# Hash attention with a PReLU layer on one core: first three weights on SyncE behind pair 1's blocks, weight 0's passes later, sums of x behind the next divide

## Chip, core and metric

The kernel runs on one core of a Trainium2 chip. A core has five engines with instruction streams of their own: TensorE (PE, matmuls), VectorE (DVE), ScalarE (ACT), GpSimd (POOL) and SyncE (SP, which here only issues DMAs). They meet through semaphores. The metric is device time in microseconds. The kernel before has a median of 879.39 us over three runs (879.0 to 880.38).

## The reference, cut to what matters

```python
# q, k, v: (4, 8, 768, 64), proj: (64, 6)
q_bits = (q @ proj > 0); k_bits = (k @ proj > 0)      # a bucket of 6 bits per row
mask = q_bucket[:, :, :, None] == k_bucket[:, :, None, :]
scores = where(mask, q @ k.T / sqrt(64), -1e9)
attn = softmax(scores); x = (attn @ v)                 # heads side by side: x is (3072, 512)
h = x @ w_in                                           # w_in (512, 2048)
g = max(h, 0) + alpha * min(h, 0)
out = g @ w_out                                        # w_out (2048, 512)
```

The weights arrive as 64-bit floats and are used as 32-bit floats.

## The kernel before

**Pairs and cells.** The 32 (batch, head) problems are taken two heads at a time, in 16 pairs: pair `pi` is batch `pi // 4`, heads `2 * (pi % 4)` and the next. The loop over pairs fills the first 325 us or so; the two matrix products with the weights fill the rest. Within a pair, `scores` (L760 to L771) goes through 12 cells: six blocks of 128 keys (`kc`) by two halves of 384 queries (`g`). A cell is six matmuls into one two-bank PSUM tile `sc`, and one exponential on ScalarE into `pt`. The tag `sc` has three such tiles, and `totals` (the sums `sm` of the softmax, L815), the transposes of the first pair and the hash products take theirs from the same three, in turn. So a pair's third cell gets the tile that the preceding pair's `sm` held, once the two `st` transposes at the head of `divide` (L831) have read it.

**Order.** `do` keeps each engine's instructions in the order in which the program lists them. All engines run strictly in that order. The steps of one turn of the loop over pairs on VectorE are:

1. `divide(pi - 1, weight_begin)`: the `st` transposes, reciprocals, then, by `weight_begin`, `turn_blocks` of the next k, the clamp and parts of weight `2 pi`, `add_first` (L779, needs the first four exponentials of the pair in the order of the loop); then `dn` and `x` (L843, L849);
2. `weight_sum` of weight `2 pi` (two operations), the clamp of the next weight, `add_third`, the two of `add_last`, and `add_total`;
3. the parts and the sum of weight `2 pi + 1`, `turn_blocks` of the q two pairs on;
4. in pairs 11, 12, 13 and 15 one of the four sums of x (`sum_x`, L874, which subtracts two blocks of x of 128 x 768).

TensorE has, in a turn: 12 cells, the hash products of the next pair, `attend` (96 matmuls, 7.96 us) and `totals`, which needs `add_total`.

**Weights.** There are 32 weight pieces of 512 KB, two a pair. `load_weight(i)` (L578 to L582) issues the load, on the POOL queue if nothing else is said, into one of three `raw` buffers. `weight_abs(i)` (L591 to L600) takes the pieces apart: a pass on ScalarE (`wr`, L596), and another on ScalarE or, if so told, on VectorE (`wx`, L598). `weight_clamp` (L606) and `weight_parts` (L612) follow on VectorE, then `weight_sum` (L637, L640). POOL makes combinations of finished pieces (L659), one for each call of `weight_sums`.

**The start.** Pair 0's q and k are loaded in two halves each: q on SP's queue, k on ScalarE's. The first half is turned by TensorE (L695), copied and hashed; so is the second. From pair 1 on, q and k come by blocks of 32 columns (`load_blocks`, L512: four DMAs of 96 KB for each, in runs of 128 bytes) and are turned by VectorE (`turn_blocks`, L704). `ahead` names the three cells of pair 0 that need only the first half of q and k. The first of them lies between the second halves' transposes and their hash products.

The order of loads on SP after setup: second half of q0; weight 0; q1; k1; v0; v1; q2; k2. Weights 1 and 2 go out on POOL's queue, which reaches them as soon as its setup is done.

```python
    load_weight(0, nc.sync)
    load(1, "q")
    load(1, "k")
    load(0, "v")
    for i in range(1, 3):
        load_weight(i)
```

Of the kernel before, what the change touches and what calls it, by code (L numbers as in the profile page):

```python
# [407 lines left out]
def fast_path(  # L408
# [12 lines left out]
    nc = tc.nc  # L421
# [22 lines left out]
    PE, DVE, ACT, POOL = nc.tensor, nc.vector, nc.scalar, nc.gpsimd  # L444
# [38 lines left out]
    def load(pi, name):  # L483
        b, hp = pairs[pi]
        src = {"q": q, "k": k, "v": v}[name]
        if name == "v":
            t = pool.tile([P, 2, NC * D], F32, name=f"vn{pi}", tag="vn")
            nc.sync.dma_start(t, src[b, 2 * hp : 2 * hp + 2].rearrange("h (p c) d -> p h (c d)", c=NC))
            nat[name, pi] = t
        elif pi and name in BY_BLOCKS:  # L490
            load_blocks(pi, name)
        else:
            load_part(pi, name, slice(0, NC), nc.sync)
# [84 lines left out]
    def load_weight(i, queue=nc.gpsimd):  # L578
        if i < NW:
            i = order[i]  # L580
            raw[i] = pool.tile([P, 512], moe_w_in.dtype, name=f"raw{i}", tag="raw", bufs=3)
            queue.dma_start(raw[i], piece(i))  # L582
# [8 lines left out]
    def weight_abs(i, engine=None):  # L591
        i = order[i]
        lo, hi = halves(i)
        wx[i] = pool.tile([P, 512], F32, name=f"wx{i}", tag="wx")
        wr[i] = pool.tile([P, 512], I32, name=f"wr{i}", tag="wr")
        do(ACT.activation(wr[i], lo, AF.Copy, scale=2.0 ** -29))  # L596
        if engine is DVE:
            do(DVE.tensor_scalar(wx[i].bitcast(U32), hi, 0x7FFFFFFF, None, op0=ALU.bitwise_and))  # L598
            return
        do(ACT.activation(wx[i], hi.bitcast(F32), AF.Abs))  # L600

    def weight_clamp(i):
        if i < NW:
            i = order[i]
            x = wx[i]
            do(DVE.tensor_scalar(x, x, HI_MIN, None, op0=ALU.max, op1=ALU.max, accum_out=wmax[:, i : i + 1]))  # L606

    def weight_parts(i):
        i = order[i]
        x = wx[i].bitcast(U32)  # L610
        turned = i < HW and i % 4 == 3
        do(DVE.tensor_scalar(  # L612
            x, x, 3, 0x40000000 if turned else 0xC0000000, op0=ALU.logical_shift_left, op1=ALU.bitwise_xor,
        ))

    def weight_sum(i):


        i = order[i]
        lo, hi = halves(i)  # L620
        x = wx[i]
        if i < HW:
            n, m = divmod(i, 4)
            if m == 0:
                wst[n] = pool.tile([P, NM, 4, P], F32, name=f"wsi{n}", tag="wsi")
            slot = (0, 5, 1, 2)[m]
            dst = wst[n][:, slot].rearrange("p i f -> p (i f)")
        else:
            n, m = divmod(i - HW, 2)
            if m == 0:  # L630
                wst[HW + n] = pool.tile([P, 4, DM // 2], F32, name=f"wso{n}", tag="wso")
            w = wst[HW + n]
            dst = w[:, 0:4:3] if m == 0 else w[:, 1:3]
        x, r = x.bitcast(I32), wr[i]
        if i >= HW:
            hi, x, r = (t.rearrange("p (a f) -> p a f", a=2) for t in (hi, x, r))
        do(DVE.scalar_tensor_tensor(  # L637
            x.bitcast(U32), hi, 0x80000000, x.bitcast(U32), op0=ALU.bitwise_and, op1=ALU.bitwise_xor,
        ))
        do(DVE.tensor_tensor(dst.bitcast(I32), x, r, op=ALU.add))  # L640
        return (dst if i < HW else dst[:, 0])[:, :1]
# [118 lines left out]
    def scores(pi, cells):  # L760
        for kc, g in cells:
            sc = two_banks(f"sc{pi}_{kc}_{g}")
            ks = slice(kc * P, (kc + 1) * P)
            qs = slice(g * CW, (g + 1) * CW)
            for what, first in ((bits, True), (tr, False)):
                for s in range(2):
                    r = slice(D * s, D * s + D)
                    do(PE.matmul(  # L768
                        sc[:, s, :CW], what["k", pi][r, ks], what["q", pi][r, qs], start=first, stop=not first,
                    ))  # L770
            do(ACT.activation(pts[kc][:, g, :, :CW], sc[:, :, :CW], AF.Exp, scale=SCALE / DOWN))  # L771
# [5 lines left out]
    def add_first(pi):  # L777
        accp[pi] = pool.tile([P, 2 * NCH, CW], F32, name=f"accp{pi}", tag="accp", bufs=1)
        do(DVE.tensor_tensor(accp[pi], p(0), p(1), op=ALU.add))  # L779
# [40 lines left out]
    def divide(pi, between=lambda: None):  # L820

        b, hp = pairs[pi]
        n = HW2 // 32
        a = pool.tile([P, NCH, HW2], F32, name=f"st{pi}", tag="st", bufs=1)
        r = pool.tile([P, NCH, n], F32, name=f"rc{pi}", tag="rc")
        rr = pool.tile([P, NCH, 2, n], F32, name=f"rr{pi}", tag="rr")
        d = pool.tile([P, NCH, CW], F32, name=f"dn{pi}", tag="dn", bufs=1)
        for g in range(NCH):  # L830
            do(DVE.transpose(a[:, g], sums[pi][:, g, :HW2]))  # L831
        do(DVE.tensor_scalar(r, a.rearrange("p g (n w) -> p g n w", w=32)[:, :, :, 0], S * EPS, None, op0=ALU.add))
        for h in range(2):
            do(DVE.reciprocal(rr[:, :, h], r))
        vsum[pi] = pool.tile([P, 1], F32, name=f"vs{pi}", tag="vs")
        do(DVE.tensor_scalar(vsum[pi], av[pi][:, 0, CW : CW + 1], EPS, None, op0=ALU.mult))
        weight_sums(1, vsum[pi])
        for q0 in (0, D):
            q1 = q0 + 32
            do(POOL.tensor_copy(rr[q0 : q0 + 32, :, 1], rr[q1 : q1 + 32, :, 1]))  # L840
            do(POOL.tensor_copy(rr[q1 : q1 + 32, :, 0], rr[q0 : q0 + 32, :, 0]))
        between()
        do(DVE.transpose(  # L843
            d.rearrange("p g w -> p (g w)"),
            rr.rearrange("p g h n -> p (g h n)").unsqueeze(2).to_broadcast([P, 2 * NCH * n, 32]),
        ))

        x = mid.tile([P, NCH, CW], F32, name=f"x{pi}", tag="x", bufs=1)
        do(DVE.scalar_tensor_tensor(x, av[pi][:, :, :CW], vsum[pi], d, op0=ALU.add, op1=ALU.mult))  # L849
        nc.sync.dma_start(x_s[b, hp], x.rearrange("p g w -> p (g w)"))  # L850
# [291 lines left out]
    for half in (first, second):  # L1142
        turn(0, "q", half)
        turn(0, "k", half, DVE)
        if half is first:
            nil[0]()
            hash_bits(0, first, DVE)
    load_weight(0, nc.sync)
    load(1, "q")
    load(1, "k")  # L1150
    load(0, "v")
    for i in range(1, 3):
        load_weight(i)
    load(1, "v")
    load(2, "q")
    load(2, "k")
# [1 line left out]
    ahead = [(kc, 0) for kc in range(CH)]  # L1158
# [3 lines left out]
    turn_blocks(1, "q")  # L1162
    turn_blocks(1, "k")

    weight_abs(0, DVE)
    weight_clamp(0)
    weight_parts(0)
    for pi in range(NPAIR):
        i = 2 * pi

        def weight_begin():
            if pi + 1 < NPAIR:
                turn_blocks(pi + 1, "k")
            weight_clamp(i)
            weight_parts(i)
            add_first(pi)

        scores(pi, [c for c in CELLS if pi or c not in ahead])
        if pi:
            divide(pi - 1, weight_begin)  # L1180
        else:
            add_first(pi)
        weight_sum(i)
        weight_group(i)
        load_weight(i + 3)
        if pi == 0:
            weight_abs(1, DVE)
        weight_clamp(i + 1)
        add_third(pi)
        add_last(pi)  # L1190
        add_total(pi)
        weight_parts(i + 1)
        weight_sums(1, weight_sum(i + 1))
        weight_group(i + 1)
        load_weight(i + 4)
        if pi + 1 < NPAIR:
            hash_bits(pi + 1)
            do(ACT.activation(tr["q", pi + 1], tr["q", pi + 1], AF.Copy, scale=DOWN))
        if pi + 2 < NPAIR:
            turn_blocks(pi + 2, "q")  # L1200
        attend(pi)
        if pi + 1 == NPAIR:
            now = ff1(0, 0)
            now.step(1)
        totals(pi)
        if pi + 1 == NPAIR:
            now.step(5)
            divide(pi)
        else:
            weight_abs(i + 2)  # L1210
        if pi + 2 < NPAIR:
            load(pi + 2, "v")
        if pi in (9, 11, 15):
            load_w((9, 11, 15).index(pi))
        if pi in (9, 10, 12):
            load_x(0, *{9: (0,), 10: (2, 3), 12: (1,)}[pi])
        if 11 <= pi < 14 or pi == 15:
            sum_x(0, min(pi - 11, 3), DVE)
        if pi == 1:
            setup_alpha()  # L1220
        for name in "qk":
            magnitude(pi, name)
            if pi + 3 < NPAIR:
                load(pi + 3, name)
        if pi + 1 < NPAIR:
            weight_abs(i + 3)
# [97 lines left out]
```

## Time and profile before

| | |
|---|---|
| median of 3 runs | 879.39 us |
| the profiled execution | 879.32 us |
| its span, first to last instruction | 877.4 us |
| mean granted TensorE clock | 0.996 |
| DMA | 137.23 MB, mean 156 GB/s |

The durations below all come from the one profiled execution. Its span leaves out 1.9 us around the instructions. A row of the time line gives start, length, engine, line, what is written from what, how often, and in brackets how long the engine had been idle and what ended that. A row of the waits gives total, number of times and the longest. Times are microseconds from the start of the span.

The first pair on VectorE, in the order of time:

| start us | what | length us |
|---|---|---|
| 14.98 | second half's bits of k (L755) | 1.37 |
| 16.38, 17.28 | `turn_blocks` of q1 and k1 | 0.98, 0.94 |
| 18.14 | `weight_abs(0)` | 0.38 |
| 18.56 | clamp of weight 0 | 0.69 |
| 19.29 | parts of weight 0 | 0.43 |
| 19.76 | `add_first(0)` | 1.76 |
| 21.44 | `weight_sum(0)` | 0.68 + 0.69 |
| 29.15 | `add_total(0)` | 1.76 |
| 33.61 | `st` of pair 0 | 0.61 |

On ScalarE the pass of weight 0 (L596, 0.68 us) starts at 17.65, after the third exponential. On TensorE, `attend(0)` starts at 24.84, `totals(0)` at 32.61 and the third cell of pair 1 at 35.01.

### The profile page before, as it was taken

Reading aid. Unit: us, or ns where it says so; the run is one execution under the profiler, and the core shown is the slowest. Engines: PE = TensorE matmul, PEld = TensorE weight load, DVE = VectorE, ACT = ScalarE, POOL = GpSimd, SP = SyncE. Lnnn points to the kernel's source line nnn. Section 1 sums busy time; section 2 is a strip of 40 time slices with the busy share of each in tenths; the row PEclk is TensorE's granted clock in tenths of the full one; section 3 lists DMA queues with packets and bytes.
Section 4 is the critical chain, followed back from the end, with each engine's and each line's share of the span. In section 5 each row is a group of like instructions: output and inputs, shape, how many; then the busy total and the mean of one; then the engine's idle time right before and its main releaser. Section 6 shows DMA issues by size and latency. Waiting matters only on the chain.

```text
span 877.4 us, 15248 instructions
## 1 busy us (share of the span) xinstructions
PE 861.8 (98%) x5706; PEld 574.8 (66%) x5706; DVE 749.7 (85%) x1215; ACT 368.5 (42%) x654; POOL 117.6 (13%) x251
## 2 busy tenths in 40 slices
PE   7999999999999999999999999999999999999996
PEld 3444444444444445559996558996558997557996
DVE  4999999999999987999897769898668889668985
ACT  5888788888777752221112222112222112222111
POOL 1223343323424401120000000000000000000000
PEclk9999999999999999999999999999999999999999
DMA  9775797898799437686434435333434433420242
GB/s 198 149 177 139 168 225 170 167 235 226 187 229 200 138 126 264 225 282 224 162 111 106 151 104 184 115 137 101 151 111 155 148 112 103 173 84 1 96 160 61
DMA packets 170819, 137.23 MB, mean 156 GB/s; under 512 B 126016, under 2 KB 154384, under 8 KB 167152
## 3 DMA queue, kind: packets, MB, share of 16 engines
q1 hardware_dynamic: 158672, 107.39, 43.2%
q0 software_dynamic: 9648, 27.60, 10.7%
q10 hardware_dynamic: 2416, 1.18, 0.5%
q8 instruction: 47, 0.77, 0.4%
q14 instruction: 36, 0.29, 0.1%
HBM read 104.87 MB, written 28.31 MB: 152 GB/s over the span
## 4 chain that ended last, share of the span: by engine, by line
PE 63%; DVE 5%; issue 1%; POOL 0%; ACT 0%; DVEq 0%; ACTq 0%
PE f_0a L902 2%; PE z_4a L902 2%; PE z_7a L902 2%; PE z_3a L902 2%; PE z_6a L902 2%; PE z_5a L902 2%; PE f_4a L902 2%; PE f_3a L902 2%; PE f_2a L902 2%; PE f_1a L902 2%; PE z_2a L902 2%; PE f_5a L902 2%; PE sc L768 2%; PE av L801 2%; PE z_1a L902 2%; PE f_7a L902 2%
## 5 line engine op out<-in xcount | busy, mean ns | idle before, releaser
L771 ACT ACTIVATE pt<-sc 128x768 f32<-128x768 f32 x192 | 154.2, 812 | 6.8 <-PE sc L768 5.3
L768 PE MATMUL sc<-qT,kT 64*128 64x384 f32 x768 | 155.8, 484 | 0.0
L801 PE MATMUL av<-pt,vn 128*32 128x385 f32 (+1 forms) x1536 | 127.4, 486 | 0.0
L801 PEld LDWEIGHTS av<-pt,vn 128*32 128x32 f32 x1536 | 48.7, 109 | 77.5 <-issue 68.7
L768 PEld LDWEIGHTS sc<-qT,kT 64*128 64x128 f32 x768 | 68.3, 188 | 37.9 <-issue 37.7
L955 DVE TENSOR_TENSOR g<-g,g 128x384 f32<-128x384 f32 x128 | 68.3, 554 | 2.2
L768 PE MATMUL sc<-qb,kb 64*128 64x384 bf16 x384 | 63.1, 324 | 2.3 <-DVE st L831 2.3
L1019 DVE TENSOR_TENSOR gs<-g,gs 128x768 f32<-128x768 f32 x56 | 53.3, 951 | 1.0
L1011 DVE TENSOR_TENSOR ws<-wl 128x512 f32<-128x512 f32 x56 | 38.4, 686 | 17.9 <-DMA wl<-w_out_s 16.1
L1019 DVE TENSOR_TENSOR gs<-g 128x768 f32<-128x768 f32 x56 | 53.2, 950 | 0.0
L596 ACT ACTIVATE wr<-raw 128x512 int32<-128x512 uint32 x32 | 22.2, 693 | 53.1 <-issue 36.3
L951 DVE SCALAR_TENSOR_TENSOR g<-h,alpha 128x384 f32<-128x384 f32 x32 | 19.7, 616 | 25.2 <-ACT h L944 25.1
L768 PEld LDWEIGHTS <-kb 64*128 64x128 bf16 x384 | 19.1, 94 | 33.2 <-issue 6.4
L779 DVE TENSOR_TENSOR accp<-pt,pt 128x1536 f32<-128x1536 f32 x16 | 28.1, 1758 | 11.2 <-ACT pt L771 11.2
L741 POOL DMA_DIRECT2D qb<-kb x60 | 30.1, 506 | 34.6 <-ACT kb L736 34.6
L784 DVE TENSOR_TENSOR accd<-accd,pt 128x1536 f32<-128x1536 f32 x16 | 28.1, 1758 | 1.7
L790 DVE TENSOR_TENSOR accd<-accd,accp 128x1536 f32<-128x1536 f32 x16 | 28.1, 1758 | 0.6
L787 DVE TENSOR_TENSOR accp<-accp,pt 128x1536 f32<-128x1536 f32 x16 | 28.0, 1752 | 0.0
L783 DVE TENSOR_TENSOR accd<-pt,pt 128x1536 f32<-128x1536 f32 x16 | 28.0, 1750 | 0.0
L902 PE MATMUL f_0a<-x,wi 128*128 128x384 f32 x64 | 23.5, 489 | 0.0
L902 PE MATMUL f_1a<-x,wi 128*128 128x384 f32 x64 | 23.3, 486 | 0.0
L902 PE MATMUL f_2a<-x,wi 128*128 128x384 f32 x64 | 23.3, 486 | 0.0
(357 smaller groups left out, 1763.4 us busy)
## 6 DMA issues: line engine op xcount, KB each, us to landing
wi<-w_in_s SPq DMA_DIRECT2D x32, 896.0 KB, 4.7
wl<-w_out_s SPq DMA_DIRECT2D x16, 1024.0 KB, 4.8
wl<-w_out_r SPq DMA_DIRECT2D x12, 1024.0 KB, 4.8
raw<-in_moe_w_in_dram POOLq DMA_DIRECT2D x16, 512.0 KB, 5.0
raw<-in_moe_w_out_dram POOLq DMA_DIRECT2D x15, 512.0 KB, 4.8
w_in_s<-wsi SPq DMA_DIRECT2D x16, 448.0 KB, 6.7
qn<-in_q_dram SPq DMA_DIRECT2D x64, 96.0 KB, 5.5
vn<-in_v_dram SPq DMA_DIRECT2D x16, 384.0 KB, 5.6
```

Source lines behind the costliest of these rows:

```text
L741: nc.gpsimd.dma_start(bits["q", pi][D * s : D * s + 32, cols], raw[c + 32 : c + 64, 2 * half])
L768: do(PE.matmul(sc[:, s, :CW], what["k", pi][r, ks], what["q", pi][r, qs], start=first, stop=not first,))
L771: do(ACT.activation(pts[kc][:, g, :, :CW], sc[:, :, :CW], AF.Exp, scale=SCALE / DOWN))
L779: do(DVE.tensor_tensor(accp[pi], p(0), p(1), op=ALU.add))
L783: do(DVE.tensor_tensor(accd[pi], p(3), p(4), op=ALU.add))
L784: do(DVE.tensor_tensor(accd[pi], accd[pi], p(5), op=ALU.add))
L790: do(DVE.tensor_tensor(accd[pi], accd[pi], accp[pi], op=ALU.add))
L801: do(PE.matmul(av[pi][D * s + t : D * s + t + 32, g, :w], nat["v", pi][:, s, kc * D + t : kc * D + t + 32], pts[kc][:, g, s, :w], start=(k ...
L902: do(PE.matmul(self.ps[bank], self.left(left, k), self.right(right, k), start=start and k == 0, stop=k == self.nk - 1, skip_group_check=no ...
L955: do(DVE.tensor_tensor(new_g(b, to)[:, i], g_m[b, x][:, i], g_m[b, y][:, i], op=ALU.subtract))
L1011: do(DVE.tensor_tensor(t, w2[b, n, x], w2[b, n, y], op=op))
L1019: do(DVE.tensor_tensor(t, g2[b, n, x], g2[b, n, y], op=ALU.subtract))
```

## The change

Three things are moved, and nothing is added to or taken from what is computed.

- Weight 0 is loaded on SP's queue behind the blocks of pair 1 instead of ahead of them. Weights 1 and 2 also go on SP's queue, behind v0, instead of POOL's.
- `weight_abs(0)` no longer stands ahead of all of pair 0's remaining nine cells, but behind four of them. Clamp and parts of weight 0 stand behind `add_first(0)` instead of ahead of it.
- The first three sums of x stood at the ends of pairs 11, 12 and 13, ahead of the next pair's `divide`. They now stand in pairs 12, 13 and 14 right behind it. The fourth stays at the end of pair 15.

```diff
-    load_weight(0, nc.sync)
     load(1, "q")
     load(1, "k")
+    load_weight(0, nc.sync)
     load(0, "v")
     for i in range(1, 3):
-        load_weight(i)
+        load_weight(i, nc.sync)
...
-    weight_abs(0, DVE)
-    weight_clamp(0)
-    weight_parts(0)
     for pi in range(NPAIR):
...
-        scores(pi, [c for c in CELLS if pi or c not in ahead])
         if pi:
+            scores(pi, CELLS)
             divide(pi - 1, weight_begin)
         else:
+            rest = [c for c in CELLS if c not in ahead]
+            scores(pi, rest[:4])
+            weight_abs(0, DVE)
+            scores(pi, rest[4:])
             add_first(pi)
+            weight_clamp(0)
+            weight_parts(0)
+        if 12 <= pi < 15:
+            sum_x(0, pi - 12, DVE)
         weight_sum(i)
...
-        if 11 <= pi < 14 or pi == 15:
-            sum_x(0, min(pi - 11, 3), DVE)
+        if pi == 15:
+            sum_x(0, 3, DVE)
```

## The prediction

> **What bounds the kernel now.** I read the page first (busy shares, chain of waits), then who TensorE waits for, then the time line and short windows around those waits, then landing times of single DMAs.
>
> ```profile
> PE 861.8 (98%) x5706; PEld 574.8 (66%) x5706; DVE 749.7 (85%) x1215; ACT 368.5 (42%) x654; POOL 117.6 (13%) x251
> ```
> TensorE is busy for 861.8 of 877.4 us, and the change touches none of its matmuls. It can only take or give back some of the 15.6 us in which TensorE stands still, or runs at a lower clock. The waits of TensorE, all of them:
>
> ```profile
> PE tp_q L695 <- DMA qn<-in_q_dram: 4.1, 1, 4.1
> PE sc L768 <- DVE st L831: 2.3, 3, 1.3
> PE nil L531 <- DVE hb L535: 1.2, 1, 1.2
> PE z_2c L902 <- DVE m L1040: 0.5, 1, 0.5
> ```
> The first two rows are the two places the change works on: the second half of pair 0's q, and the sums of x ahead of `divide`. The start, by windows (columns: length, busy of PE, PEld, DVE, ACT, POOL, granted clock, DMA share, GB/s):
>
> ```profile
> 4.00:6.66 2.66, 2.60 (x20) 1.05 (x19) 0.56 (x1) 0.93 (x3) 0.06 (x1) 1.00 0.94 239
> 6.66:10.72 4.06, 0.00 (x1) 0.03 (x1) 0.68 (x1) 0.92 (x2) 0.00 (x0) 1.00 1.07 330
> 10.72:14.20 3.48, 3.48 (x18) 1.75 (x24) 0.56 (x1) 0.90 (x2) 0.00 (x0) 0.53 0.88 109
> ```
> TensorE idles for 4.06 us while the DMA engines move 330 GB/s, which is the weights; then it works 3.5 us at half clock. So this gap costs twice. The issues around it:
>
> ```profile
> 2.81 0.69 POOL L582 DMA_DIRECT2D raw<-in_moe_w_in_dram  x1
> 3.50 0.55 POOL L582 DMA_DIRECT2D raw<-in_moe_w_out_dram  x1
> 3.96 0.95 SPq L501 DMA_DIRECT2D qn<-in_q_dram  x2
> 4.95 0.49 SPq L582 DMA_DIRECT2D raw<-in_moe_w_out_dram  x1
> 5.49 6.51 SPq L512 DMA_DIRECT2D qn<-in_q_dram  x4
> 12.04 2.77 SPq L512 DMA_DIRECT2D kn<-in_k_dram  x4
> ```
> Two weights of 512 KB are ahead of q's second half and a third is right behind it. That half landed 6.1 to 6.2 us after issue; the first half, without weights in the way, took 2.5 to 3.2.
>
> The second place, pairs 12 and 14:
> ```profile
> 244.58 1.61 DVE L874 TENSOR_TENSOR x<-x,x 128x768 f32<-128x768 f32 x1
> 246.11 0.63 DVE L831 STREAM_TRANSPOSE st<-sm 128x192 f32<-128x192 f32 x2
> ...
> 246.80 0.34 PE L768 MATMUL sc<-qb,kb 64*128 64x384 bf16 x2 [0.86 <-DVE st L831]
> ...
> 286.91 0.34 PE L768 MATMUL sc<-qb,kb 64*128 64x384 bf16 x2 [1.29 <-DVE st L831]
> ```
> A pair's third cell needs the PSUM tile that `sm` holds until VectorE's two `st` transposes have read it. A sum of x just ahead of `st` makes TensorE wait.
>
> **What the Trainium skill says.** TensorE: Matmul & The Clock Gate, part 1: an idle window of about 3.4 us halves the clock, and it comes back after a busy one. The trace agrees: 4.06 us idle, then 0.50 from about 10.9 to 14.3. DMA: Bandwidth & Descriptors, "Issuing engines are not separate DMA queues": queues of POOL and SP interleave on the same engines. That fits the q half that weights of another queue hold up. SBUF — State Buffer, "Who interferes with whom": a VectorE operation with two SBUF inputs excludes a GpSimd one that reads SBUF. The trace agrees: the sum of x took 1.61 us in pairs 12 and 14, where POOL's L659 ran, and 0.92 in pair 13, where it didn't.
>
> **Part 1, the loads at the start.** Removed: two weight issues from POOL (0.69 and 0.55 us, POOL idle afterwards until 22.67: worth nothing as such) and 1.5 MB of DMA ahead of or beside q's second half. SP now issues, behind that half (ends 4.91): four blocks of q1, four of k1, weight 0, v0, weights 1 and 2.
> - q's second half: its second DMA is issued at about 4.5; with the first half's 2.5 to 3.2 us it lands at 7.0 to 7.7. I take 7.2, against 10.72: 3.5 us. TensorE then idles 0.5 us, so I take the clock as 1.00 throughout.
> - At full clock transposes take 0.85 (4.33 to 5.18 in the first half), cell 1 takes 0.81, hash 0.83 (5.83 to 6.66). Cell 2 starts at 9.7. Before, it was 14.78. TensorE alone could be 5.1 us earlier, 1.55 of it from the clock.
>
> What is late next: VectorE is in order, and now has pair 1's k (`turn_blocks`) and then weight 0's `weight_abs` ahead of `add_first`.
> - An unhindered block issue takes 0.66 us (k1 before). Eight from 4.95 end at 10.3; in the run before q2 and k2 took 8 us for eight behind big loads. Between these, I let k1 end at 10.4 to 11.2. k1 lands up to 3.5 us after its last issue, 13 to 14, and VectorE turns it until 14 to 15.
> - Weight 0 is issued after it and lands at R. The one weight load near the start without much company took 4.7 us (issue 22.67), in company 7.3. The fastest weight load of the trace took 3.8. So R lies between 10.4 + 3.8 = 14.2 and 11.2 + 4.7 = 15.9; I take 15.0, about the middle.
> - `weight_abs` takes 0.42 with its gap, so `add_first` starts at A = R + 0.42 = 15.45. Its own data (five exponentials) are there by about 14.2.
> - Before, `add_first` started at 19.76 and the `st` of pair 0 ended at 34.22, 14.46 later. The clamp and parts of weight 0 now lie inside this stretch: 18.56 to 19.72 before, 1.16. So `st` ends at A + 15.62, and the third cell of pair 1, at 35.01 before, can't start sooner than 0.05 after. The gain of the start is S = 19.34 - A, at most 5.1: with A = 15.45, **3.9 us**. `totals` would allow 20.25 - A, so `st` decides.
> - ScalarE's part of `weight_abs` (0.69) now stands behind the seventh exponential, at about 15.3 to 15.6 with TensorE early; R = 15.0 doesn't hold it. Later R costs about the same as on VectorE.
>
> Hidden, with the cover: SP's added issues (about 1.0 us) push v0, needed by `attend(0)` at 20.9, landing by about 16.2; weight 1 at the latest 19.3, needed at 19.6; weight 2 19.8, needed at 23; q2 and k2 about 26, needed at 28.8 and 30.8. The bits of pair 1 (last issue 29.46 before, 25.6 now) share the DMA with q2 and k2: landing was 1.6 to 3.3 in that place, 5.8 at most anywhere; scores of pair 1 need them at 29.5. At 5.8 this costs 1.9.
>
> **Part 2, the sums of x.** Cost before, by the step from cell 2 to cell 3, 0.81 undisturbed: pair 12 1.83, pair 13 1.15, pair 14 2.26, so 1.0 + 0.35 + 1.45 = 2.8 us. In pair 1 `st` ended at 53.59 and cell 3 started at 54.31, so VectorE has about 0.65 us to spare. 1.61 - 0.65 and 0.92 - 0.65 give the first two; in pair 14 `dn` came 0.4 late too, from POOL's long `rr` copy (1.71).
>
> Behind `divide` each sum should take 0.92, since POOL ran no tensor operation there (248.6 to 254.4 is idle). But VectorE doesn't wait for anything between `accp` and `st`, so the delay still arrives at the `st` one pair later: pair 13 0.92 - 0.65 = 0.3, pair 14 0.3 to 0.75 with the late `dn`, pair 15 about 0, as it has no `turn_blocks` (0.97) left. `totals` has 1.39 us spare (262.17 to 263.56), 0.98 with late `dn`: enough for 0.92. New loss about 1.1, gain **1.7 us**. Bounds: 0 if the sums meet POOL and take 1.61, 2.8 if nothing is left. The loads of x for these sums were done two pairs earlier, so nothing waits for data.
>
> Sum: 3.9 + 1.7 = 5.6 off the profiled execution's 879.32 (span 877.4 and 1.9 around it; the median is 879.39, so no correction): **873.7 us**.
>
> **Rivals.** A measurement of this kernel tells about 0.2% (1.8 us) from no change.
> - *The weight takes the place of the q wait.* The blocks of 128 bytes fill SP's queue, R is 17: A = 17.4, S = 1.9, and of the sums 1.1 is gained: 876.3. For it: q1's four issues took 6.51 us. Against it: weight 0 was ahead of them then.
> - *The moves only shift the waits.* R = 18, S = 0.9, sums nothing: 878.4. For it: VectorE has nearly no slack in pairs 12 to 14.
> - *Slower: weight 0 holds up VectorE and ScalarE.* If q1's issues keep their 6.51 us with no weights ahead (to 11.46), k1 2.77 (to 14.2) and weight 0 its 7.3, R = 21.5, A = 21.9, S = -2.6; with no gain from the sums 881.9. The start loses from R = 18.9 on. Against it: k1's issues, without a weight ahead, took 0.66 each.
>
> **How the numbers follow.** Forecast 0.56 (own range 871.5 to 875.3, from R = 13.8 to 16, with the sums' 0.8 to 2.8), weight in q's place 0.24, waits only shifted 0.13, slower 0.07. The range 871.3 to 877.2 takes in the first two. Faster by over 0.2% 0.80, within 0.14, slower 0.06: a part of the slower case ends within 0.2%.
>
> **What would show it.** tp_q's wait under 1 us and a granted clock of 1.00 from 10 to 15; cell 2 near 9.7; weight 0 landing near 15 and `add_first` right behind its `weight_abs`; third cell of pair 1 near 31. L874 at 0.92 three times, waits for `st` in pairs 13 and 14 of under 0.8 each. I'd be wrong if q's half lands after 9 all the same, if SP's block issues stay at 6.5 us, or if `sm` starts to wait for VectorE in pairs 12 to 14.

## The result

The changed kernel takes 873.87 us (median, 873.72 to 874.04, four runs) against 879.35 before (879.0 to 880.38, four runs): a ratio of 0.9936, 95% interval 0.9919 to 0.9953. The two profiled executions took 879.32 and 874.04, with spans of 877.4 and 872.3. The forecast was 873.7.

First the engine shares of the changed kernel's page, then all waits of TensorE (total, times, longest):

```profile
PE 861.0 (99%) x5706; PEld 575.2 (66%) x5706; DVE 748.5 (86%) x1215; ACT 366.8 (42%) x654; POOL 116.2 (13%) x249
```
```profile
PE sc L768 <- DVE st L831: 1.4, 3, 0.6
PE nil L531 <- DVE hb L535: 1.2, 1, 1.2
PE tp_q L695 <- DMA qn<-in_q_dram: 0.5, 1, 0.5
PE z_2c L902 <- DVE m L1040: 0.5, 1, 0.5
PE sc L768 <- ACT pt L771: 0.3, 1, 0.3
PE sm L815 <- DVE accd L790: 0.2, 1, 0.2
```
TensorE's work is the same within 0.8 us; its waits are what changed. The wait for q went from 4.1 to 0.5 us, the one for `st` from 2.3 to 1.4. Two rows are new: an exponential (0.3) and `add_total` (0.2).

The windows of the start (length, busy of PE, PEld, DVE, ACT, POOL, granted clock, DMA share, GB/s) have 0.48 us of idle time left, from 6.66 to 8.00, and no half clock any more:

```profile
4.00:6.66 2.66, 2.62 (x20) 1.32 (x19) 0.56 (x1) 0.86 (x2) 0.00 (x0) 1.00 0.56 123
6.66:8.00 1.34, 0.86 (x9) 0.54 (x6) 0.68 (x1) 1.15 (x2) 0.00 (x0) 1.00 0.84 134
8.00:11.00 3.00, 3.00 (x32) 1.31 (x31) 1.39 (x3) 2.14 (x4) 0.00 (x0) 1.00 0.90 141
11.00:14.20 3.20, 3.20 (x26) 1.75 (x24) 2.32 (x3) 3.18 (x5) 0.00 (x0) 1.00 0.98 220
```
The DMA carries small q and k runs at 123 to 141 GB/s until 11 us, where it used to carry the weights. SP's issues in the time line:

```profile
4.07 0.95 SPq L501 DMA_DIRECT2D qn<-in_q_dram  x2
5.07 2.79 SPq L512 DMA_DIRECT2D qn<-in_q_dram  x4
7.90 2.77 SPq L512 DMA_DIRECT2D kn<-in_k_dram  x4
10.71 0.66 SPq L582 DMA_DIRECT2D raw<-in_moe_w_out_dram  x1
```
q1's four issues fell from 6.51 to 2.79 us. What is late next shows on VectorE:

```profile
13.38 0.98 DVE L704 STREAM_TRANSPOSE kT<-kn 128x768 f32<-128x768 f32 x1 [0.85 <-DMA kn<-in_k_dram]
15.16 0.43 DVE L598 TENSOR_SCALAR wx<-raw 128x512 uint32<-128x512 uint32 x1 [0.80 <-DMA raw<-in_moe_w_out_dram]
15.50 1.75 DVE L779 TENSOR_TENSOR accp<-pt,pt 128x1536 f32<-128x1536 f32 x1
...
30.64 0.60 DVE L831 STREAM_TRANSPOSE st<-sm 128x192 f32<-128x192 f32 x2
```
VectorE waits for k1 and then for weight 0. Its time line shows no further wait until `st`. TensorE's third cells of pairs 1, 13 and 14 wait for `st`; the row at 301.98 is the fourth cell of pair 15, which waits for an exponential:

```profile
31.31 0.34 PE L768 MATMUL sc<-qb,kb 64*128 64x384 bf16 x2 [0.64 <-DVE st L831]
...
261.57 0.34 PE L768 MATMUL sc<-qb,kb 64*128 64x384 bf16 x2 [0.17 <-DVE st L831]
...
281.47 0.34 PE L768 MATMUL sc<-qb,kb 64*128 64x384 bf16 x2 [0.54 <-DVE st L831]
...
301.98 0.34 PE L768 MATMUL sc<-qb,kb 64*128 64x384 bf16 x2 [0.33 <-ACT pt L771]
...
318.73 0.86 PE L815 MATMUL sm<-accd,ones 128*32 128x192 f32 x16
```
Before, the third cell of pair 1 and the last `sm` stood here:

```profile
35.01 0.33 PE L768 MATMUL sc<-qb,kb 64*128 64x384 bf16 x2
...
323.61 0.86 PE L815 MATMUL sm<-accd,ones 128*32 128x192 f32 x16
```
The third cell of pair 1 starts at 31.31 instead of 35.01: 3.7 us from the start. At the last `sm` of pair 15 (323.61 before, 318.73 now) the lead is 4.9: the sums brought 1.2. The spans differ by 5.1 us and the two executions by 5.3. These last 0.4 us come after pair 15 or from outside of the span, where the change moves nothing; their cause is open.

### The profile page after: what moved, and what is told of

It reads as the page before. It is cut to its first block, busy times and chain, and to the rows that moved or that the text cites. A ratio compares the mean times of both kernels' runs of the same rounds, so it can differ in the third digit from the quotient of the medians.

```text
span 872.3 us, 15248 instructions
## 1 busy us (share of the span) xinstructions
PE 861.0 (99%) x5706; PEld 575.2 (66%) x5706; DVE 748.5 (86%) x1215; ACT 366.8 (42%) x654; POOL 116.2 (13%) x249
## 4 chain that ended last, share of the span: by engine, by line
PE 65%; DVE 1%; issue 1%; POOL 0%; ACT 0%; DVEq 0%
PE f_0a L902 2%; PE z_4a L902 2%; PE z_6a L902 2%; PE z_7a L902 2%; PE z_3a L902 2%; PE z_2a L902 2%; PE z_1a L902 2%; PE z_5a L902 2%; PE f_4a L902 2%; PE f_2a L902 2%; PE f_5a L902 2%; PE f_7a L902 2%; PE f_6a L902 2%; PE f_3a L902 2%; PE f_1a L902 2%; PE z_2c L902 1%
```

## The experiments

Times come from several chips, on which the kernel before took 880.3, 880.24 and 880.71 us in the three sets. So the ratio to the kernel before, run beside each, is what counts; the last column is that ratio on 879.35, for comparison with the expectations. The ratio need not equal the quotient of the medians named here to the last digit. The traces named below are of one execution each.

| kernel | median us | ratio (95%) | on 879.35 |
|---|---|---|---|
| start only | 875.82 | 0.9952 (0.9938 to 0.9965) | 875.1 |
| sums only | 879.15 | 0.9991 (0.9983 to 0.9998) | 878.6 |
| loads only | 877.55 | 0.9973 (0.9963 to 0.9983) | 877.0 |
| passes only | 879.54 | 0.9989 (0.9981 to 0.9998) | 878.4 |
| weights 1, 2 left on POOL | 878.92 | 0.9984 (0.9978 to 0.9991) | 877.9 |
| weight 0 left ahead of the blocks | 876.20 | 0.9947 (0.9934 to 0.9960) | 874.7 |
| before, with TensorE kept busy | 880.48 | 1.0003 (0.9994 to 1.0011) | 879.6 |
| changed, `add_first` ahead of the pass | 874.37 | 0.9928 (0.9916 to 0.9941) | 873.0 |
| changed, sums in gaps | 873.00 | 0.9913 (0.9899 to 0.9926) | 871.7 |
| changed, both of these | 872.75 | 0.9915 (0.9901 to 0.9928) | 871.9 |
| changed, again | 874.69 | 0.9933 (0.9920 to 0.9947) | 873.5 |

My theory: two independent parts, 3.7 us at the start and 1.25 at the sums; the start is set by when `add_first` of pair 0 can begin on VectorE, so by k1 and weight 0. The rivals: the parts depend on each other, the place of the passes doesn't matter, or the clock is what pays.

**The parts alone.** Start only:

```diff
-        if 12 <= pi < 15:
-            sum_x(0, pi - 12, DVE)
...
-        if pi == 15:
-            sum_x(0, 3, DVE)
+        if 11 <= pi < 14 or pi == 15:
+            sum_x(0, min(pi - 11, 3), DVE)
```


> The start's part of the change alone; the sums of x stay where they were. Theory (two independent parts: the start is worth what the third cell of pair 1 comes earlier, 3.7 us, and the sums about 1.25 us): 875.6 us, third cell of pair 1 at about 31.3, and in pairs 12 to 14 the same steps from cell 2 to cell 3 as before, 1.83, 1.15 and 2.26 us. Rival (the two parts share their gain, the lead of the start is lost again at the old sums or the sums only pay because of the lead): either near 874.0 or above 876.5.

Sums only:

```diff
         if pi:
             divide(pi - 1, weight_begin)
         else:
             add_first(pi)
+        if 12 <= pi < 15:
+            sum_x(0, pi - 12, DVE)
...
-        if 11 <= pi < 14 or pi == 15:
-            sum_x(0, min(pi - 11, 3), DVE)
+        if pi == 15:
+            sum_x(0, 3, DVE)
```


> The move of the sums of x alone; the start stays as it was. Theory: gain 1.25 us, 878.1 us: steps from cell 2 to cell 3 of 0.81, 1.15 and 1.5 us in pairs 12 to 14, and in pair 15 a new wait of 0.5 us for an exponential. Rival (the gain of the sums is the full 2.8 us and something else was lost in the changed kernel): 876.6 us. Rival (it only shifts waits): 879.3 us.

Start only gained 4.2 us (3.1 to 5.5), sums only 0.8 (0.2 to 1.5): together 5.0 against 5.6 (4.1 to 7.1) for the whole, so nothing speaks for a tie between them. The third cell of pair 1, expected at 31.3, came at 32.17 in the profiled execution of the start only, as k1 and weight 0 came later there. With the start only, the old waits for `st` are all there; with the sums only, the new ones:

```profile
243.99 0.34 PE L768 MATMUL sc<-qb,kb 64*128 64x384 bf16 x2 [0.88 <-DVE st L831]
263.49 0.34 PE L768 MATMUL sc<-qb,kb 64*128 64x384 bf16 x2 [0.18 <-DVE st L831]
284.09 0.33 PE L768 MATMUL sc<-qb,kb 64*128 64x384 bf16 x2 [1.28 <-DVE st L831]
```
```profile
265.06 0.34 PE L768 MATMUL sc<-qb,kb 64*128 64x384 bf16 x2 [0.18 <-DVE st L831]
284.96 0.34 PE L768 MATMUL sc<-qb,kb 64*128 64x384 bf16 x2 [0.54 <-DVE st L831]
305.47 0.34 PE L768 MATMUL sc<-qb,kb 64*128 64x384 bf16 x2 [0.33 <-ACT pt L771]
```
The first fence is the start only (pairs 12, 13, 14), the second the sums only (13, 14, 15): within 0.02 us the same three numbers as in the kernels before and after.

**Loads and passes.** Loads only is the kernel before with the changed order of loads; passes only has the changed place of weight 0's passes and the old loads (each the respective hunk of the change).

> Only the order of the loads is changed; weight 0's passes stay ahead of pair 0's remaining cells, and the sums stay. Theory (the landing of weight 0, about 15.1, now holds ScalarE and VectorE ahead of the fourth exponential): TensorE waits for sc tiles in pair 0, the start gains about 2.7 us instead of 3.7: 876.7 us. Rival (the place of the passes doesn't matter, since VectorE waits for weight 0 either way): 875.6 us.

> Only the place of weight 0's passes is changed; loads and sums stay. Theory (TensorE's wait for q and the half clock set the start, the passes weren't in the way): 879.2 us, within 0.4 of before, tp_q still waits 4 us. Rival (the passes held up the exponentials and their move is a good part of the gain): 878.2 us or less.

The loads alone gained 2.4 us (1.5 to 3.3). TensorE's wait of 4.1 us for q is gone, and a wait of 2.4 for an exponential has come in its place, as the theory had it; the waits for `st` are those of before:

```profile
PE sc L768 <- ACT pt L771: 2.4, 1, 2.4
PE sc L768 <- DVE st L831: 2.3, 3, 1.3
```
ScalarE's pass waits for weight 0 with nine exponentials queued behind it:

```profile
15.37 0.67 ACT L596 ACTIVATE wr<-raw 128x512 int32<-128x512 uint32 x1 [2.39 <-DMA raw<-in_moe_w_out_dram]
```
With the passes moved too (start only), that wait of TensorE is gone. What this is worth is less sure: the gains of 2.4 (1.5 to 3.3) and 4.2 (3.1 to 5.5) have intervals that overlap a little, and in the two profiled executions the third cell of pair 1 came at 32.71 and 32.17, 0.5 apart. The passes alone gave 1.0 us (0.2 to 1.7), nearer to the rival than to the theory's 0.15. But in the profiled execution the third cell of pair 1 came at 35.20, no earlier than before, and k1 was turned only at 18.19 (17.28 before). So where that gain comes from isn't shown. No run moves ScalarE's pass without VectorE's.

**Which weight held up q.** Both are the changed kernel with one thing put back:

```diff
     for i in range(1, 3):
-        load_weight(i, nc.sync)
+        load_weight(i)
```


> The changed kernel, but with weights 1 and 2 on POOL's queue as before; weight 0 stays behind the blocks. Theory (the two weights of the other queue hold up the second half of q, weight 0 behind it on the same queue doesn't): tp_q waits 4 us and the clock goes to half again, the start gains about 0.2 us and the sums 1.25: 877.9 us. Rival (weight 0 on SP's own queue was what held it up): tp_q waits under 1 us, 874 us.

```diff
+    load_weight(0, nc.sync)
     load(1, "q")
     load(1, "k")
-    load_weight(0, nc.sync)
```


> The changed kernel, but with weight 0 right behind the second half of q, ahead of the blocks, as before; weights 1 and 2 on SP's queue behind v0. Theory: tp_q waits 0.5 us as in the changed kernel, the clock stays full; the blocks come 1.5 us later, k1 lands near 14.5 to 15, and VectorE turns it until 15.5 to 16, so that add_first starts near 16.4 and the start gains 2.9 instead of 3.7: 874.8 us. Rival (weight 0 also holds up the second half of q): tp_q waits 2 us or more, 876 us or above.

With weights 1 and 2 on POOL the wait for q and the half clock are back; the first fence has the wait, the second the window at half clock:

```profile
PE tp_q L695 <- DMA qn<-in_q_dram: 3.4, 1, 3.4
```
```profile
10.72:14.20 3.48, 3.11 (x18) 1.69 (x24) 0.56 (x1) 0.62 (x2) 0.00 (x0) 0.60 0.80 126
```
The gain of 1.4 us (0.8 to 1.9) is what the sums bring, plus nearly nothing. The two DMAs of q's second half took 6.5 us (median) from issue to landing here and 6.1 before; with weights 1 and 2 behind v0 they took 2.6 with weight 0 ahead of the blocks and 2.5 in the changed kernel. With weight 0 ahead of the blocks, q has no wait left among TensorE's rows, but k1 comes late:

```profile
15.58 0.98 DVE L704 STREAM_TRANSPOSE kT<-kn 128x768 f32<-128x768 f32 x1 [1.94 <-DMA kn<-in_k_dram]
16.48 0.39 DVE L598 TENSOR_SCALAR wx<-raw 128x512 uint32<-128x512 uint32 x1
16.79 1.75 DVE L779 TENSOR_TENSOR accp<-pt,pt 128x1536 f32<-128x1536 f32 x1
```
`add_first` starts 1.29 us later than in the changed kernel, and the third cell of pair 1 1.28 later (32.59). So the weights of the other queue held up q, and weight 0 on q's own queue held up k1. That k1's turn came at 15.58 is more than scatter, as it started between 13.38 and 14.43 in the seven executions with the blocks first. In the time this second step doesn't show: the ratios of this kernel (0.9947) and of the changed one (0.9936) have intervals that overlap widely. The other queue also held up q1: its four issues on SP took 5.83 us with only weights 1 and 2 ahead, 4.00 with only weight 0 ahead, 6.51 with all three and 2.79 with none.

**The clock.** The kernel before, with TensorE kept busy while it waits for q (`zero_w[0]` is the tile of zeros from setup; the transposes overwrite the product):

```diff
         ps = two_banks(f"tp_{name}{pi}")
+        if halves.start == 1 and name == "q":
+            for i in range(14):
+                do(PE.matmul(ps[:, 0], zero_w[0][:, :P], zero_w[0], start=True, stop=True))
```


> The kernel before, with 14 more matmuls of zeros (nil) ahead of the second half's transposes of q, in the time in which TensorE waits for q. They change no output. Theory (the half clock costs TensorE 1.55 us, but VectorE has only about 0.7 us to spare at the st of pair 0 while k1 lands at 17): clock 1.00 from 10 to 15, cell 2 near 13.2 instead of 14.78, and 878.6 us. Rival (the whole 1.55 us of the clock come out at the end): 877.8 us. Rival (clock costs nothing here): 879.3 us.

The clock stayed at 1.00, and the time didn't fall (1.0003; 878.8 to 880.3 on 879.35). That fits the rival in which the clock costs nothing (879.3) and neither of the other two. But q itself landed later in the profiled execution (tp_q at 12.01, 10.72 before), so this run alone doesn't settle it. The sums-only kernel says more: in its profiled execution q came at 10.67, as before, but the clock stayed full.

```profile
11.00:14.30 3.30, 3.30 (x33) 1.61 (x33) 1.50 (x3) 2.26 (x4) 0.00 (x0) 1.00 1.00 122
```
There cell 2 started at 13.15, 1.6 us earlier than the 14.78 of before; the third cell of pair 1 at 34.73, 0.28 earlier. k1 had come at 17.82, and VectorE had waited 1.95 us for it. So in that execution the clock's 1.55 us came to 0.3. With VectorE as it was before they could hardly have given more than about 0.7, an estimate from that trace: `st` ended there at 34.22, and the third cell started at 35.01.

**Where VectorE could be freed.** VectorE's pass of weight 0 goes behind `add_first`; ScalarE's stays ("first" issues ScalarE's pass alone, "second" VectorE's):

```diff
             scores(pi, rest[:4])
-            weight_abs(0, DVE)
+            weight_abs(0, DVE, "first")
             scores(pi, rest[4:])
             add_first(pi)
+            weight_abs(0, DVE, "second")
             weight_clamp(0)
```


> The changed kernel, with VectorE's pass of weight_abs(0) moved behind add_first of pair 0; ScalarE's pass stays. Theory (the landing of weight 0 holds up VectorE's whole chain by the idle 0.80 us ahead of the pass): add_first starts near 14.4 behind k1's turn, the st of pair 0 ends 0.7 us earlier, and the third cell of pair 1 comes at 30.65: 873.2 us. Rival (ScalarE's pass, or the bits of pair 1, hold up the start just behind): 873.9 us.

```profile
13.48 0.98 DVE L707 STREAM_TRANSPOSE kT<-kn 128x768 f32<-128x768 f32 x1 [1.03 <-DMA kn<-in_k_dram]
14.38 1.71 DVE L782 TENSOR_TENSOR accp<-pt,pt 128x1536 f32<-128x1536 f32 x1
16.02 0.41 DVE L601 TENSOR_SCALAR wx<-raw 128x512 uint32<-128x512 uint32 x1
```
The wait for weight 0 is gone and the third cell of pair 1 came at 30.62, where 30.65 was expected. The ratio, 0.9928, is 0.0008 below that of the change, but the intervals overlap widely: the step is shown in the trace, its worth in the time isn't.

The sums, then both, and the changed kernel again for comparison:

```diff
             weight_clamp(i)
             weight_parts(i)
+            if pi == 12:
+                sum_x(0, 0, DVE)
             add_first(pi)
...
-        if 12 <= pi < 15:
-            sum_x(0, pi - 12, DVE)
+        if pi == 15:
+            sum_x(0, 1, DVE)
+            sum_x(0, 2, DVE)
```


> The changed kernel, with the three sums of x put where VectorE is idle: the first ahead of add_first of pair 12 (0.82 us of waiting for an exponential there), the second and third both behind the divide in pair 15, which has no turn_blocks left. Theory (the sums cost 1.55 us in the changed kernel, 0.35 and 0.7 at the third cells of pairs 13 and 14 and 0.5 at an exponential in pair 15, because VectorE has no slack there): no wait for st in pairs 13 to 15 and at most 0.2 us elsewhere, a ratio about 0.0016 below that of the changed kernel run beside it. Rival (the waits only move once more, to totals or to pair 15's exponentials): the same ratio within 0.0005, with new rows among TensorE's waits.

> The sums in the gaps and VectorE's pass of weight_abs(0) behind add_first of pair 0, both on the changed kernel. Theory: 0.7 from the start and 1.5 us from the sums, 2.2 us or a ratio about 0.0025 below the changed kernel run beside it. Rival (only one of the two counts): 0.0008 or 0.0016.

> The changed kernel as it is, for comparison on the same chip. Theory: ratio to the kernel before 0.9936 as measured, within 0.001; the third cell of pair 1 within 1 us of 31.3, depending on when k1 and weight 0 land in that execution.

With the sums in the gaps the runs took 872.52 to 873.27 us, those of the changed kernel on the same chip 874.34 to 874.92: 1.7 us less in the medians, and the ranges don't meet. In the time line of VectorE the first sum now fills what was a wait of 0.82 us, and the two in pair 15 run back to back:

```profile
244.18 0.95 DVE L874 TENSOR_TENSOR x<-x,x 128x768 f32<-128x768 f32 x1
245.08 1.76 DVE L779 TENSOR_TENSOR accp<-pt,pt 128x1536 f32<-128x1536 f32 x1
...
306.49 1.82 DVE L874 TENSOR_TENSOR x<-x,x 128x768 f32<-128x768 f32 x2
```
One wait of 0.18 for `st` is left in pair 14, and none for an exponential. Both together took 872.75, 1.9 us less than the changed kernel beside it, where 2.2 were expected, and 0.25 less than the sums in gaps alone, where 0.7 were expected. These runs can't tell the last two apart. The third cell of pair 1 was only 0.3 us ahead of that of the sums in gaps (31.27 and 31.57): TensorE was 0.35 later in that execution (cell 2 at 10.61 and 10.26), and `add_first` waited 0.29 us for an exponential. Either is faster than the changed kernel and the one before.

## Why the prediction was right, and where it wasn't

| step of the prediction | predicted | measured |
|---|---|---|
| q's second half is there | 7.2 | 7.49, 0.48 wait |
| clock from 10 to 15 | 1.00 | 1.00 |
| cell 2 | 9.7 | 9.97 |
| weight 0 lands (R) | 15.0 | about 15.1 |
| `add_first` (A) | 15.45 | 15.50 |
| third cell of pair 1 | 31.1 | 31.31 |
| gain of the start | 3.9 | 3.70 |
| a sum of x behind `divide` | 0.92 | 0.95 |
| loss at the third cells, pairs 13 and 14 | 0.3; 0.3 to 0.75 | 0.35; 0.70 |
| loss in pair 15 | about 0 | 0.49 |
| gain of the sums | 1.7 | 1.2 |

The start went as worked out, with VectorE's chain as the limit and not TensorE. The chain shows in the profiles through very different arrivals. Times are in us:

| kernel | cell 2 | k1 turned | `add_first` | third cell of pair 1 | difference of the last two |
|---|---|---|---|---|---|
| sums only | 13.15 | 17.82 | 20.22 | 34.73 | 14.51 |
| TensorE kept busy | 14.50 | 18.75 | 21.14 | 35.66 | 14.52 |
| passes only | 14.25 | 18.19 | 19.39 | 35.20 | 15.81 |
| weights 1, 2 on POOL | 15.15 | 17.65 | 19.54 | 35.35 | 15.81 |
| weight 0 ahead | 9.86 | 15.58 | 16.79 | 32.59 | 15.80 |
| start only | 10.35 | 14.43 | 16.36 | 32.17 | 15.81 |
| changed | 9.97 | 13.38 | 15.50 | 31.31 | 15.81 |
| `add_first` ahead of the pass | 9.89 | 13.48 | 14.38 | 30.62 | 16.24 |

The prediction had 14.51 with the old order and 15.67 with the clamp and parts inside. Of the 0.14 it missed, 0.12 lies between the starts of the two operations of `weight_sum` (0.72 before, 0.84 now). Cell 2 moves by 5 us between the rows; the third cell follows `add_first` to within 0.05 us wherever VectorE's order is the same. The last row has the pass inside as well, 0.43 more. The three last runs agree: 15.82 with the sums in gaps, 15.81 for the change again, and 16.29 with both. With weights 1 and 2 on POOL `add_first` itself had waited 0.64 for an exponential, so there the late TensorE came through. In the loads-only kernel and before, the difference is 15.25, and the third cell has no wait: there TensorE was last, not VectorE.

How near the numbers came is partly luck. With the same order of loads `add_first` started at 15.75, 15.78 and 16.36 in three other executions (sums in gaps, the change again, start only) against 15.50 here, so by the traces the start was worth 2.8 to 3.7 us. And the forecast gain of 5.6 was met (5.5 by the medians) although the two parts add up to 4.9 in the trace: that the sums were taken for 0.5 too much was in part made good by the 0.4 us after pair 15 and outside of the span, of which the prediction says nothing. Two of its sums are a little off: 15.0 and 0.42 are 15.42, not 15.45, and its own range from R = 13.8 to 16 comes to 871.4 to 875.6. Neither bears on the forecast.

The size that was off is in the sums: "pair 15 about 0, as it has no `turn_blocks` (0.97) left". That was right for `st`: in pair 15 the third cell came on time (0.81 after the second). But a sum behind `divide` also delays what follows on VectorE, up to the pair's second `weight_sum`. ScalarE's pass of the next weight but one reuses a buffer that this `weight_sum` reads, and the exponentials of the next pair are queued behind that pass. In the changed kernel the pass starts at 299.99, 0.94 after the first cell of pair 15, where before it was 0.12 after (304.56 and 304.44). First the pass before, then in the changed kernel, there with the pass one pair earlier (280.08):

```profile
304.56 0.68 ACT L596 ACTIVATE wr<-raw 128x512 int32<-128x512 uint32 x1 [3.96 <-issue]
```
```profile
280.08 0.69 ACT L596 ACTIVATE wr<-raw 128x512 int32<-128x512 uint32 x1 [4.83 <-DVE wso L640]
...
299.99 0.68 ACT L596 ACTIVATE wr<-raw 128x512 int32<-128x512 uint32 x1 [4.82 <-issue]
300.58 0.65 ACT L600 ACTIVATE wx<-raw 128x512 f32<-128x512 f32 x1
301.14 2.19 ACT L771 ACTIVATE pt<-sc 128x768 f32<-128x768 f32 x3
```
So the fourth cell waited for the first exponential, 1.30 us after the third instead of 0.81. In pair 15 the row names only "issue", but one pair earlier it names `weight_sum` (L640). And in pair 15 the pass starts 0.08 to 0.09 us after L640 ends in the kernel before, the changed kernel, the sums only and the sums in gaps alike (304.48 and 304.56, 299.90 and 299.99 in the first two). That the wait comes from the sums is shown, as it is there with the sums only and gone with the sums in the gaps. In pairs 13 and 14 the third cell is late itself, for `st`, and the fourth follows it after 0.82 us, so nothing of this is added there.

The rival in which the weight takes the place of q's wait needed weight 0 to land at 17; VectorE had it at 15.16. The rival in which waits only shift is refuted: sums in old and new place differ by 0.8 us (0.2 to 1.5). The slower one needed SP's block issues to stay at 6.5 us; they fell to 2.79.

## What to carry to other kernels

A long wait of the busiest engine is worth only what the next late arrival leaves: before pricing it, list everything that the engines further on need in order, and date each arrival. Loads that nobody needs for 10 us should be issued behind those that somebody waits for, on whatever queue, and the first operation that needs them should stand behind work whose data is already there. A moved operation delays all that stands behind it on its engine; follow each of those to the buffers that it frees, not only to the wait that it was moved away from.

## What I hadn't expected of the hardware

Nearly equal waits for q left the clock full in one execution and halved it in another. A wait of 3.39 us (sums only) left it at 1.00. Waits of 3.40 (weights 1 and 2 on POOL), 3.61 (passes only) and 4.06 us (before) were followed by 0.50, which began 0.3, 1.2 and 0.2 us after TensorE was back at work. Four executions are too few to tell where the limit lies. And the arrival of k1 moves by about 1 us with the same order of loads: its turn started between 13.38 (the change) and 14.43 (start only) in the seven executions that share it.
